# Moving the second product's seven small matrix products into one column group

## The chip, the cores and the metric

One core of one Trainium2 chip runs the whole program. The metric is device microseconds of one execution, as the median of several runs.

## The reference

```python
# x: (8, 4096, 192), weight: (8, 7)
w = softmax(weight, axis=-1)                        # 7 taps for each of 8 heads
out = einsum('hk,bskhg->bshg', w, x_unf)            # causal convolution along the sequence
# then, with x = out as (32768, 192), w_in: (192, 2048), w_out: (2048, 192)
h = x @ w_in
g = h * clip(h + 3.0, 0.0, 6.0) / 6.0
return g @ w_out                                    # (32768, 192), float32
```

A seven-tap convolution along the sequence is followed by two dense layers with a hard-swish gate between them.

## The kernel before, in words

The 32,768 tokens are cut into 32 blocks of 1,024, two halves of 512 tokens each. Block 0 has a form of its own. Blocks 1 to 31 each run `first_layer` and then `second_layer`; blocks 1 to 30 are the steady blocks, and block 31 takes the branches marked `last`. The convolution of a later block, on VectorE and ScalarE, is spread between the steps of the current one.

The first layer (`first_layer`, matmuls at L512) makes sixteen units of 128 hidden columns each. Each unit fills two PSUM banks; ScalarE (L303) and VectorE (L307) turn it into the gated values in the tile `g` and give the banks back. PSUM has eight banks, used as four slots of two.

The second layer (`second_layer`) multiplies `g` with `w_out`. The product is cut into seven smaller products by a Strassen-like scheme (`prod`, numbered 1 to 7: sums of blocks of `g` against sums of blocks of `w_out`). The result of one product has 96 rows, three thirds of 32. For products 1, 2, 4 and 5 two of the thirds are cut once more by the same scheme, into seven small products each; the remaining third is done plainly.

All these matmuls have 32 output rows, so TensorE runs them in four column groups, 0 to 3, side by side. Group j writes the 32 PSUM partitions from 32j on, called `first`, `second`, `third` and `fourth` in the code; such a strip of a bank is a quadrant here. The order is written out by hand as a plan of 80 steps per group. A plain matmul has 512 columns and takes two steps, a short one (of a small product) has 256 and takes one; each is an fp32 matmul and leaves two passes in the trace. These are the helpers:

- `plain(j, bank, n, q, chunks, start)` puts matmuls of product n, third q, into group j's strip of a bank, one for each of the eight chunks of `g`.
- `small(n, m, out, start, j)` puts the four short matmuls of small product m of product n.
- `level_two(n, p, order, j)` puts small products in the given order, into four strips of half a bank (`chains[j]`: A, E, B, C), and queues for each the copy that it needs: A to B after the first, B to C after the sixth, and copies to the SBUF tile of the product after the others.
- `fill(k)` puts k plain matmuls of the third third of product 5 into group 3, bank `a`.
- `do(t, fn)` queues work of the other engines (copies on ScalarE, sums on VectorE, transfers on GpSimd) at step t, half a step early. All streams are then sorted by step, and this is the order of the instructions on each engine; within one engine nothing overtakes.

The bank names: `x_, b`, `y_, c` and `a, _` are the three slots that the first layer gives back first, `f, h` the fourth. `x_` and `y_` hold the strips A, E and B, C of `level_two`. `b` collects products 6 and 3 on top of product 1 (and holds plain thirds early on), `c` product 7. Where one bank of PSUM is copied to another (`copy`, on ScalarE) matmuls go on adding to the copy. The framework sets the semaphores; a matmul waits for a copy or a sum by a count of the engine's finished instructions, and two instructions that touch one bank can be put in order in this way even where their partitions differ.

In the steady blocks before, the pieces of the second product stand in all groups: small products 1, 7, 2 and 4 in group 0, 5 in group 1, 3 in group 2 and 6 in group 3, with copies from strip to strip between them (`B2`, `C2`, `D2`), and its plain third in group 3. The plain third of product 4 stands in group 0, at the start of bank `b`.

Lines that matter: L512 first-layer matmuls, L640 second-layer matmuls, L637 the copies queued by `do(..., copy, ...)`, L730 to L735 the six copies of `level_two` (in the order first, second, sixth, fifth, seventh, third small product), L817 to L819 and L857, L858 the copies of product 2 to SBUF, L557 a negation on ScalarE ahead of an accumulating transfer, L588, L415 and L459 sums. L849 and L930 copy finished products, L1078 and L477 are the first multiplication of the next convolution and the first part of the split of `y`.

Of the kernel before, what the change touches and what calls it, by code (L numbers as in the profile page):

```python
# [25 lines left out]
def kernel(  # L26
# [16 lines left out]
    N = 512  # L43
    G = 2
    TB = G * N
    D2 = P // 2
# [41 lines left out]
    for base, dma in ((0, nc.scalar), (D2, nc.sync)):  # L88
        dma.dma_start(
            out=w_sb[base : base + D2],  # L90
            in_=weight.unsqueeze(1).to_broadcast([H, GJ, KC]),
# [126 lines left out]
    for n in range(AHEAD):  # L218
# [8 lines left out]
        out=e_sb[:], in0=w_sb[:], in1=mx[:].to_broadcast([P, KC]), op=ALU.subtract  # L227
# [54 lines left out]
    def take():  # L282
        return free_banks.pop(0)
# [72 lines left out]
    every = range(NP)  # L356
# [90 lines left out]
    def rows(q):  # L447
        return slice(q * QS, (q + 1) * QS)
# [9 lines left out]
    def add(out, x, y, op=ALU.add):  # L458
        nc.vector.tensor_tensor(out=out, in0=x, in1=y, op=op)  # L459
# [112 lines left out]
    halves = slice(0, TH), slice(TH, N)  # L572

    def four_parts(x):
        return [x[:, c::2, t] for t in halves for c in range(2)]
# [14 lines left out]
    def quarters(w):  # L590
        return [
            w_out[:, c::2, w, q * QS : (q + 1) * QS] for c in range(2) for q in range(2)
        ]
# [12 lines left out]
    def second_layer(i, between):  # L606
        last = i + 1 == NB
        ours = [free_slots.pop(0) for _ in range(3)]
        x_, b, y_, c, a, _ = (psum[:, 2 * n + k] for n in ours for k in range(2))
# [3 lines left out]
        copy = nc.scalar.copy  # L613
        m = slice(0, DH)
        lo, hi = halves
        both = nc.sync, nc.scalar
        first, second, third, fourth = (rows(q) for q in range(4))
        f, h = (psum[:, 2 * free_slots[0] + k] for k in range(2))
        end = h
        V = a[fourth]  # L620
        chains = {
            j: [bank[rows(j), t] for bank in (x_, y_) for t in halves] for j in (1, 2, 3)
        }
        A2, E2, C2, D2 = f[first, lo], f[second, hi], h[first, lo], h[third, hi]
        B2 = h[second if last else fourth, hi]
        j1 = 3 if last else 1
        late = {}

# [3 lines left out]
        def put(j, cost, fn):  # L632
            streams[j].append((clock[j], fn))
            clock[j] += cost

        def do(t, fn, *args, **kw):
            streams[3].append((t - 0.5, lambda: fn(*args, **kw)))  # L637

        def matmul(j, out, w, x, start):
            nc.tensor.matmul(  # L640
                out=out, lhsT=w, rhs=x, start=start, stop=True,
                tile_position=(0, j * QS), skip_group_check=True,
            )

        def plain(j, bank, n, q, chunks, start=False):
            x, w = prod[n]
            x = S3 if x is None else x
            for k, ch in enumerate(chunks):
                put(j, 2, lambda ch=ch, k=k: matmul(
                    j, bank[rows(j)], w_out[:, ch, w, q * QS : (q + 1) * QS], x[:, ch],  # L650
                    start and k == 0,
                ))
# [8 lines left out]
        def small(n, m_, out, start=False, j=3):  # L661

            x, w = prod[n]
            sums, ws = {
                1: (shared, w_s[:, 0]), 5: (s5, w_s[:, 1]), 2: (sums2, w_s[:, 2]),
                4: (sums4[0], w_s[:, 3]),
            }[n]
            x11, x12, x21, x22 = four_parts(x)
            z1, z2, z3, z4 = four_parts(sums)
            b11, t3, b21, b22 = quarters(w)  # L670
            t1, t2, t4 = (ws[:, k] for k in range(3))
            xm, wm = {
                1: (x11, b11), 2: (x12, b21), 3: (z4, b22), 4: (x22, t4),
                5: (z1, t1), 6: (z2, t2), 7: (z3, t3),
            }[m_]
            for u in range(NP // 2):
                put(j, 1, lambda u=u: matmul(
                    j, out, wm[:, u], xm[:, u], start and u == 0
                ))
# [16 lines left out]
        def fold(p, m136):  # L696
            add(p[second, hi], p[second, hi], p[second, lo])
            add(p[second, lo], m136, p[second, lo])
# [11 lines left out]
        def p2(r, t):  # L710
            return late["p2"][r, t]

        def p3(q):
            if last:
                plain_by_halves(q, 3, q, 0)
                plain_by_halves(q, 3, q, 1)
            else:
                plain(q, b, 3, q, in_fours)
# [6 lines left out]
        p4 = Fourth()  # L725

        def level_two(n, p, order, j=3):
            A, E, B, C = chains[j]
            steps = {
                1: lambda: copy(out=B, in_=A),  # L730
                2: lambda: copy(out=p()[first, lo], in_=A),
                6: lambda: copy(out=C, in_=B),
                5: lambda: copy(out=p()[second, lo], in_=E),
                7: lambda: copy(out=p()[second, hi], in_=C),
                3: lambda: copy(out=p()[first, hi], in_=C),  # L735
            }
            to = {1: A, 2: A, 6: B, 5: E, 7: C, 3: B, 4: C}
            for k in order:
                small(n, k, to[k], k in (1, 5), j)
                if k != 4:  # L740
                    late_by = {(1, 2): 8.1, (4, 2): 8.2 if last else 19.3}.get((n, k), 0.02 if n == 4 else 0)
                    do(clock[j] + late_by, steps[k])

        rest = 6, 2, 7, 5, 4, 3
        chunks, first_fill = list(every), [True]

        def fill(k):
            plain(3, a, 5, 2, [chunks.pop(0) for _ in range(k)], first_fill.pop() if first_fill else False)
# [2 lines left out]
            for ch in every[2:6]:  # L751
                by_half(3, (a, c)[t], 2, 2, ch, t)

        plain(0, b, 4, 2, every, True)
        small(2, 1, A2, True, 0)
        plain(0, c, 7, 0, every, True)
        small(2, 7, C2, False, 0)
        small(2, 2, A2, False, 0)
        plain(0, b, 6, 0, every)
        small(2, 4, C2, False, 0)  # L760
        p3(0)

        if last:
            plain(1, b, 1, 2, every, True)
            plain(1, c, 7, 1, every[:4], True)
            plain(1, a, 2, 2, every[:2], True)
            small(2, 6, B2, False, 1)
            plain(1, c, 7, 1, every[4:])
            small(2, 5, E2, True, 1)
            plain(1, b, 6, 1, every)  # L770
            plain(1, a, 2, 2, every[6:])
        else:
            level_two(1, lambda: p1, (1,), 1)
            plain(1, c, 7, 1, every[:4], True)
            level_two(1, lambda: p1, rest, 1)
            plain(1, c, 7, 1, every[4:])
            plain(1, b, 6, 1, every)
            small(2, 5, E2, True, 1)
        p3(1)

        level_two(4, lambda: p4, (1,), 2)
# [2 lines left out]
        level_two(4, lambda: p4, rest, 2)  # L784
        plain(2, c, 7, 2, every[ahead:])
        plain(2, b, 6, 2, every)
        small(2, 3, D2, False, 2)
        p3(2)

        if last:  # L790
            level_two(1, lambda: p1, (1,))
            fill(2)
            level_two(1, lambda: p1, rest)
            fill(4)
        else:
            plain(3, b, 1, 2, every, True)
            plain(3, c, 2, 2, every[:6], True)
            small(2, 6, B2, False)
            plain(3, c, 2, 2, every[6:])
            fill(4)  # L800
        level_two(5, lambda: late["p5"], (1,))
        fill(2)
        level_two(5, lambda: late["p5"], rest)
# [5 lines left out]
        assert clock == [80] * 4  # L809

        for t in halves:
            do(30 if t == hi else 29, copy, out=p4[third, t], in_=b[first, t])
        do(25.5, copy, out=p1[third], in_=b[second if last else fourth])
        do(20, copy, out=B2, in_=A2)
        do(31.9, copy, out=C2, in_=B2)
        do(39.6, copy, out=D2, in_=B2)
        do(40, lambda: copy(out=p2(second, hi), in_=C2))  # L817
        do(44, lambda: copy(out=p2(first, lo), in_=A2))
        do(44 if last else 64, lambda: copy(out=p2(second, lo), in_=E2))  # L819

        for t, job in between:
            do(t, job)
# [31 lines left out]
        if last:  # L854
            do(49, lambda: copy(out=late["p5"][third], in_=V))
        else:
            do(56.6, lambda: copy(out=p2(third, slice(0, N)), in_=c[fourth]))  # L857
        do(64.4, lambda: copy(out=p2(first, hi), in_=C2))  # L858
        if last:
            do(64.4, lambda: add(p2(third, slice(0, N)), a[second], p1[third]))  # L860
            for bank, t in ((a, lo), (c, hi)):
                do(64.4, lambda bank=bank, t=t: copy(out=bank[fourth, t], in_=p2(third, t)))
        do(64.4, lambda: fold(late["p2"], D2))
        whole = slice(0, 2 * QS if last else DH)
        do(64.6, lambda: add(late["p2"][whole], late["p2"][whole], p1[whole]))
        if last:
# [92 lines left out]
    with tc.manual_schedule():  # L959
# [4 lines left out]
            out=c_sb[:], in0=e_sb[:], in1=sm[:].to_broadcast([P, KC]), op=ALU.mult  # L964
# [14 lines left out]
        b = take()  # L979
        for cols in (N, N, N // 2):  # L980

            nc.tensor.matmul(  # L982
                out=psum[:, b, 0:cols], lhsT=zeros[:, 0:P], rhs=zeros[:, 0:cols],
# [59 lines left out]
        n = 3  # L1043
        for slot, (c, group) in enumerate(parts):
            first = slot < len(early)
# [27 lines left out]
        late = ctx.enter_context(tc.tile_pool(name="late", bufs=1, reuse_waits="tile"))  # L1073
# [60 lines left out]
        last = ctx.enter_context(tc.tile_pool(name="last", bufs=1, reuse_waits="tile"))  # L1134
# [55 lines left out]
```

## Time and profile before

| what | value |
|---|---|
| median of 3 runs | 2195.47 us (2195.26 to 2195.56) |
| the profiled execution | 2195.6 us, its span 2193.8 us |
| TensorE matmuls | 2188.3 us busy, 100% of the span |
| VectorE, ScalarE, GpSimd busy | 89%, 56%, 54% of the span |
| granted TensorE clock | 1.00 |
| one second layer, 1479.66 to 1514.21 | 34.55 us: VectorE busy 30.39, ScalarE 20.57, GpSimd 12.96 |
| one first layer, 1446.80 to 1479.66 | 32.86 us: VectorE busy 30.16, ScalarE 17.38, GpSimd 24.26 |

The profile is one execution. Starts and ends are microseconds from its beginning. Matmul ends in it are modelled, since matmuls are pipelined, so starts are compared with starts. The chain is the list of work that ended last, followed back from the end; a wait names the instruction that released it.

### The profile page before, as it was taken

The numbers are of one execution on the slowest core, as the hardware profiler recorded it, in microseconds if no ns is written. First come the engines' busy times: TensorE is split into PE (matmuls) and PEld (weight loads), VectorE is DVE, ScalarE is ACT, GpSimd is POOL, SyncE is SP. The second block draws the span as 40 slices with busy tenths as digits, with TensorE's granted clock in tenths as the row PEclk, the third lists the DMA queues.
The fourth block names the chain that finished last, engine by engine and source line by source line (L and its number), as shares of the span: only waits on it lengthen the run. The fifth ranks groups of instructions, "written<-read, shape, count | busy, mean of one in ns | idle before, by whom it ended". The sixth has DMA issues, their size and how long they took to land.

```text
span 2193.8 us, 53991 instructions
## 1 busy us (share of the span) xinstructions
PE 2188.3 (100%) x22984; PEld 1501.9 (68%) x22984; DVE 1953.5 (89%) x1956; ACT 1230.1 (56%) x1800; POOL 1178.8 (54%) x1028
## 2 busy tenths in 40 slices
PE   9999999999999999999999999999999999999999
PEld 4467776677766677766777667776667776677766
DVE  8888998898998889988899888999888998899977
ACT  7355565554555655555546555455565555554654
POOL 2456654565544666445655456554456554565544
PEclk9999999999999999999999999999999999999999
DMA  6277778777778777797777878777877778777776
GB/s 159 60 138 146 147 147 151 141 146 145 148 139 157 141 139 146 147 159 131 147 147 145 148 145 145 145 146 145 159 135 139 147 148 154 135 147 144 135 143 112
DMA packets 352434, 312.59 MB, mean 142 GB/s; under 512 B 211904, under 2 KB 264640, under 8 KB 352192
## 3 DMA queue, kind: packets, MB, share of 16 engines
q0 software_dynamic: 114640, 233.87, 59.3%
q1 hardware_dynamic: 235624, 74.66, 16.9%
q8 instruction: 180, 2.95, 0.6%
q10 hardware_dynamic: 1928, 0.59, 0.1%
q14 instruction: 62, 0.51, 0.1%
HBM read 31.72 MB, written 25.17 MB: 26 GB/s over the span
## 4 chain that ended last, share of the span: by engine, by line
PE 100%; DVE 0%; issue 0%
PE psum L640 49%; PE psum L512 46%; PE psum L297 2%; PE psum L342 2%; PE psum L974 0%; PE psum L982 0%; PE psum L895 0%; DVE zeros L111 0%; DVE shared L922 0%; DVE x L96 0%; DVE half L233 0%; DVE bias_e L150 0%; DVE bias_e L149 0%
## 5 line engine op out<-in xcount | busy, mean ns | idle before, releaser
L640 PE MATMUL psum<-g,w_out 128*32 128x512 f32 (+1 forms) x5960 | 922.8, 503 | 0.0
L303 ACT ACTIVATE g<-psum,half 128x1024 f32<-128x1024 f32 (+1 forms) x528 | 574.4, 1092 | 485.6 <-PE psum L512 485.6
L307 DVE SCALAR_TENSOR_TENSOR g<-g,psum 128x1024 f32<-128x1024 f32 (+1 forms) x528 | 608.2, 1180 | 106.4 <-ACT g L303 106.1
L640 PE MATMUL psum<-s,w_out 128*32 128x512 f32 (+1 forms) x3024 | 657.9, 585 | 0.0
L640 PEld LDWEIGHTS psum<-g,w_out 128*32 128x32 f32 x5960 | 375.0, 110 | 248.9 <-issue 116.0
L512 PE MATMUL psum<-y_own,w_in 64*128 64x512 f32 x4464 | 515.1, 388 | 0.0
L512 PE MATMUL psum<-y_other,w_in 64*128 64x512 f32 x4464 | 510.9, 386 | 0.0
L512 PEld LDWEIGHTS psum<-y_own,w_in 64*128 64x128 f32 x4464 | 415.8, 184 | 112.1 <-issue 26.0
L512 PEld LDWEIGHTS psum<-y_other,w_in 64*128 64x128 f32 x4464 | 418.1, 184 | 87.8
L588 POOL TENSOR_TENSOR shared<-g,shared 128x256 f32<-128x256 f32 x248 | 358.0, 1444 | 54.8 <-DVE g L307 29.0
L1080 DVE SCALAR_TENSOR_TENSOR y<-x,c_sb,y 128x1536 f32<-128x1536 f32 x186 | 334.7, 1799 | 0.2
L554 POOL DMA_DIRECT2D s<-g x123 | 147.1, 1198 | 266.4 <-PE psum L640 123.5
L640 PE MATMUL psum<-g,w_s 128*32 128x256 f32 x1488 | 282.3, 379 | 0.0
L640 PEld LDWEIGHTS psum<-s,w_out 128*32 128x32 f32 x3024 | 197.2, 110 | 74.0 <-issue 16.0
L554 POOL DMA_DIRECT2D g<-g x124 | 180.8, 1519 | 106.7 <-DVE s L415 106.7
L640 PE MATMUL psum<-z,w_s 128*32 128x256 f32 x992 | 228.1, 379 | 0.0
L640 PE MATMUL psum<-z,w_out 128*32 128x256 f32 x992 | 227.2, 379 | 0.0
L459 DVE TENSOR_TENSOR g<-g 128x1024 f32<-128x1024 f32 x124 | 148.7, 1220 | 44.5 <-PE psum L640 44.5
L588 POOL TENSOR_TENSOR shared<-g 128x256 f32<-128x256 f32 x124 | 92.0, 742 | 171.4 <-DVE g L307 171.4
L640 PEld LDWEIGHTS psum<-g,w_s 128*32 128x32 f32 x1488 | 138.0, 110 | 42.7
L266 POOL DMA_DIRECT2D y_other<-y_own x90 | 48.0, 534 | 213.2 <-DVE shared L459 213.1
L554 POOL DMA_DIRECT2D z<-g x62 | 95.8, 1545 | 116.3 <-ACT z L557 116.3
(118 smaller groups left out, 2706.4 us busy)
## 6 DMA issues: line engine op xcount, KB each, us to landing
y_other<-y_own POOLq DMA_DIRECT2D x180, 384.0 KB, 8.1
g<-g POOLq DMA_DIRECT2D x124, 512.0 KB, 6.0
s<-g POOLq DMA_DIRECT2D x123, 512.0 KB, 6.4
z<-g POOLq DMA_DIRECT2D x62, 512.0 KB, 7.2
out_dram<-shared SPq DMA_DIRECT2D x376, 64.0 KB, 3.9
x<-in_x_dram SPq DMA_DIRECT2D x53, 388.5 KB, 5.7
z<-g SPq DMA_DIRECT2D x31, 512.0 KB, 3.3
stage<-in_moe_w_in_dram SPq DMA_DIRECT2D x16, 192.0 KB, 5.0
```

Of the source, the lines that this page charges most:

```text
L266: dma.dma_start(out=to[D2:P], in_=part[0:D2])
L297: nc.tensor.matmul(out=psum[:, b], lhsT=w[r], rhs=src, start=start, stop=stop, skip_group_check=onto,)
L303: nc.scalar.activation(r6, h, ACT.Relu, bias=half[:], scale=1.0 / 6.0)
L307: nc.vector.scalar_tensor_tensor(out=g_, in0=g_, scalar=1.0, in1=h, op0=ALU.min, op1=ALU.mult)
L342: lambda p=p: nc.tensor.matmul(out=bank[j * QS : (j + 1) * QS, tokens], lhsT=w_out[:, p, w, cols], rhs=x[:, p, tokens], start=(first and p ...
L459: nc.vector.tensor_tensor(out=out, in0=x, in1=y, op=op)
L512: nc.tensor.matmul(out=psum[:, 2 * slots[n] + k], lhsT=r32(w_in_parts[part][r, c, s]), rhs=r32(y_other[0][r, part, s] if group else y_own[ ...
L554: nc.gpsimd.dma_start(out=out, in_=x, accum_op=ALU.add)
L588: engine.tensor_tensor(out=o, in0=p, in1=q, op=op)
L640: nc.tensor.matmul(out=out, lhsT=w, rhs=x, start=start, stop=True, tile_position=(0, j * QS), skip_group_check=True,)
L1080: jobs.append(lambda k=k: nc.vector.scalar_tensor_tensor(out=y[:], in0=x[:, :, k : k + N], scalar=c_sb[:, k : k + 1], in1=y[:], op0=ALU.mu ...
```

## The change

In the steady blocks the seven small products of the second product all go to column group 0, from step 12 on, by `level_two` with strips in `f` and `h`. What stood there moves: the plain third of product 4 starts with two chunks in group 0, bank `x_`, and is copied to `a[fourth]`, where group 3 adds the other six; of the plain third of product 5 two chunks are done in group 1, and of that of product 2 two chunks in group 2, each in its own strip of bank `a`, with copies of 512 columns that carry the partial sums from strip to strip. In each group there are then 28 short matmuls; before there were 16, 32, 32 and 32. The last block keeps its order.

```diff
+        chains[0] = [bank[first, t] for bank in (f, h) for t in halves]
...
-        B2 = h[second if last else fourth, hi]
+        B2 = h[second, hi]
...
-                    late_by = {(1, 2): 8.1, (4, 2): 8.2 if last else 19.3}.get((n, k), 0.02 if n == 4 else 0)
+                    late_by = {
+                        (1, 2): 8.1, (4, 2): 8.2 if last else 19.3, (2, 2): 8, (2, 7): -0.05, (2, 5): 4,
+                    }.get((n, k), 0.02 if n == 4 else 0)
                     do(clock[j] + late_by, steps[k])
...
-        plain(0, b, 4, 2, every, True)
-        small(2, 1, A2, True, 0)
-        plain(0, c, 7, 0, every, True)
-        small(2, 7, C2, False, 0)
-        small(2, 2, A2, False, 0)
-        plain(0, b, 6, 0, every)
-        small(2, 4, C2, False, 0)
+        if last:
...
+        else:
+            plain(0, x_, 4, 2, every[:2], True)
+            plain(0, c, 7, 0, every[:4], True)
+            level_two(2, lambda: late["p2"], (1,), 0)
+            plain(0, c, 7, 0, every[4:])
+            level_two(2, lambda: late["p2"], rest[:5], 0)
+            plain(0, b, 6, 0, every)
+            level_two(2, lambda: late["p2"], rest[5:], 0)
         p3(0)
...
             plain(1, b, 6, 1, every)
-            small(2, 5, E2, True, 1)
+            plain(1, a, 5, 2, every[4:6])
         p3(1)
...
-        small(2, 3, D2, False, 2)
+        if last:
+            small(2, 3, D2, False, 2)
+        else:
+            plain(2, a, 2, 2, every[6:])
         p3(2)
...
             plain(3, b, 1, 2, every, True)
+            plain(3, a, 4, 2, every[2:])
             plain(3, c, 2, 2, every[:6], True)
-            small(2, 6, B2, False)
-            plain(3, c, 2, 2, every[6:])
-            fill(4)
+            fill(2)
+            chunks[2:4] = []
         level_two(5, lambda: late["p5"], (1,))
         fill(2)
...
-            do(30 if t == hi else 29, copy, out=p4[third, t], in_=b[first, t])
+            do(30 if t == hi else 29, copy, out=p4[third, t], in_=(b[first, t] if last else a[fourth, t]))
...
-        do(20, copy, out=B2, in_=A2)
-        do(31.9, copy, out=C2, in_=B2)
-        do(39.6, copy, out=D2, in_=B2)
-        do(40, lambda: copy(out=p2(second, hi), in_=C2))
-        do(44, lambda: copy(out=p2(first, lo), in_=A2))
-        do(44 if last else 64, lambda: copy(out=p2(second, lo), in_=E2))
+        if last:
...
+        else:
+            do(4.2, copy, out=a[fourth], in_=x_[first])
+            do(44.05, copy, out=a[third], in_=c[fourth])
+            do(52.1, copy, out=a[second], in_=a[fourth])
+            do(64.5, copy, out=a[fourth], in_=a[second])
...
-            do(56.6, lambda: copy(out=p2(third, slice(0, N)), in_=c[fourth]))
-        do(64.4, lambda: copy(out=p2(first, hi), in_=C2))
+            do(64.4, lambda: copy(out=p2(third, slice(0, N)), in_=a[third]))
+        if last:
+            do(64.4, lambda: copy(out=p2(first, hi), in_=C2))
...
-        do(64.4, lambda: fold(late["p2"], D2))
+        do(64.4, lambda: fold(late["p2"], D2 if last else chains[0][2]))
```

In the changed kernel all lines after L624 stand one to 22 lines further down: the second-layer matmuls are L641, the queued copies L638, those of `level_two` L731 to L736.

More of the change, by code (lines that the diff above doesn't have):

```diff
@@ L752, in last_third @@
                 by_half(3, (a, c)[t], 2, 2, ch, t)
-        plain(0, b, 4, 2, every, True)
-        small(2, 1, A2, True, 0)
-        plain(0, c, 7, 0, every, True)
-        small(2, 7, C2, False, 0)
-        small(2, 2, A2, False, 0)
-        plain(0, b, 6, 0, every)
-        small(2, 4, C2, False, 0)
+        if last:
+            plain(0, b, 4, 2, every, True)
+            small(2, 1, A2, True, 0)
+            plain(0, c, 7, 0, every, True)
+            small(2, 7, C2, False, 0)
+            small(2, 2, A2, False, 0)
+            plain(0, b, 6, 0, every)
+            small(2, 4, C2, False, 0)
+        else:
[4 more added lines that the diff above has]
+            level_two(2, lambda: late["p2"], rest[:5], 0)
+            plain(0, b, 6, 0, every)
+            level_two(2, lambda: late["p2"], rest[5:], 0)
         p3(0)
@@ L811, in second_layer @@
         for t in halves:
-            do(30 if t == hi else 29, copy, out=p4[third, t], in_=b[first, t])
+            do(30 if t == hi else 29, copy, out=p4[third, t], in_=(b[first, t] if last else a[fourth, t]))
         do(25.5, copy, out=p1[third], in_=b[second if last else fourth])
-        do(20, copy, out=B2, in_=A2)
-        do(31.9, copy, out=C2, in_=B2)
-        do(39.6, copy, out=D2, in_=B2)
-        do(40, lambda: copy(out=p2(second, hi), in_=C2))
-        do(44, lambda: copy(out=p2(first, lo), in_=A2))
-        do(44 if last else 64, lambda: copy(out=p2(second, lo), in_=E2))
+        if last:
+            do(20, copy, out=B2, in_=A2)
+            do(31.9, copy, out=C2, in_=B2)
+            do(39.6, copy, out=D2, in_=B2)
+            do(40, lambda: copy(out=p2(second, hi), in_=C2))
+            do(44, lambda: copy(out=p2(first, lo), in_=A2))
+            do(44, lambda: copy(out=p2(second, lo), in_=E2))
+        else:
[3 more added lines that the diff above has]
+            do(64.5, copy, out=a[fourth], in_=a[second])
         for t, job in between:
```

## The prediction

> **What bounds the kernel now.** I read the page's busy times and its chain first, then the chain in order of time, then who the TensorE waited for.
>
> ```profile
> PE 2188.3 (100%) x22984; PEld 1501.9 (68%) x22984; DVE 1953.5 (89%) x1956; ACT 1230.1 (56%) x1800; POOL 1178.8 (54%) x1028
> PE 100%; DVE 0%; issue 0%
> ```
> ```profile
> 1446.87 32.86 PE psum L512 x288
> 1479.73 34.55 PE psum L640 x290
> ```
> ```profile
> PE psum L982 <- DVE half L233: 1.5, 1, 1.5
> ```
>
> The kernel is one unbroken stream of matmuls. In the chain every steady block is 32.86 us of first layer (L512) and 34.55 us of second layer (L640), 67.41 together. The third fence is the whole answer to "what did TensorE wait for": 1.5 us at the start, nothing in the blocks. So every other engine has slack today, no gain can come from a wait removed, and a cost comes only from a new wait of TensorE, times 30 steady blocks.
>
> Within one second layer (the block whose L640 starts at 1479.66) I read the passes of the matmuls (each fp32 matmul leaves two records):
>
> ```profile
> 1484.85 0.38 PE L640 MATMUL psum<-shared,w_s 128*32 128x256 f32 x1
> 1484.85 0.59 PE L640 MATMUL psum<-g,w_out 128*32 128x512 f32 x1
> ...
> 1485.07 0.38 PE L640 MATMUL psum<-shared,w_s 128*32 128x256 f32 x1
> ...
> 1485.28 0.38 PE L640 MATMUL psum<-shared,w_s 128*32 128x256 f32 x1
> 1485.28 0.59 PE L640 MATMUL psum<-g,w_out 128*32 128x512 f32 x1
> ...
> 1486.36 0.38 PE L640 MATMUL psum<-shared,w_s 128*32 128x256 f32 x1
> ```
>
> Starts count here, not the modelled ends. A long pass follows its predecessor in the same column group after 0.429 us (eight passes from 1481.42 to 1484.85), a short one after 0.2157 (seven, 1484.85 to 1486.36). One step of the plan is one long pass or two short ones: 0.4290 or 0.4314. The groups run independently: the long group is not slowed by the short one beside it.
>
> **TensorE's own work.** The change keeps 80 steps in each group and 112 short matmuls in all; it moves them from 16, 32, 32 and 32 per group to 28 in each. A short matmul costs 0.4314 - 0.4290 = 0.0024 us more than its step, so the slowest group loses 4 x 0.0024 = 0.01 us per block, 0.3 us over 30 blocks. That is the whole gain: -0.3 us. The Trainium skill, TensorEngine Tiling (Array Packing), Instruction Overhead, speaks of some 60 cycles of overhead for each matmul; eight passes fewer at that price would be an estimated 0.2 us per block, 6 us in all. The rows above have a fixed cost of 0.0024 and not 0.025 per pass, so the measurement decides.
>
> **Operands needed earlier.** From the VectorE timeline of the same block: the gate of the last unit (L307, 1480.92 + 1.22) ends at 1482.14, and small product 1 of the second product needs it at step 12, 1484.85. The last S3 chunks (L415) end at 1484.41, and are now needed at steps 16 and 20 (1486.6, 1488.3) instead of 28. The first of the z sums (L588, the pair at 1486.71) ends at 1487.9, now needed at step 24 (1490.0). The z sum at 1488.99 ends at 1490.2, now needed at step 36 (1495.2) instead of 60. The smallest cover is 2.1 us: cost nothing. The orders of VectorE, GpSimd and SyncE are the same instruction by instruction, so no DMA and no queue but ScalarE's and TensorE's is moved.
>
> **ScalarE.** Per block four copies of 512 columns come in (nearest row: L637 z<-psum 32x512, 0.58 us) and one copy of 256 goes (0.34), three copies more. ScalarE is busy 20.57 of the 34.55 us, so the sum fits; what counts is where it is dense. TensorE waits on ScalarE's count at certain matmuls, and the order of the changed kernel as built shows these waits. I compared each with the ScalarE row that it needs, shifted by what is now queued ahead:
> - step 20 (groups 1, 2), second of the two L732 copies: now 1487.54, one 0.37 copy ahead makes 1487.91; due 1488.30.
> - step 44, group 0, p1's copy into the bank (1497.05 + 0.57) and group 3, L731 of product four (1497.92): both 0.34 later, 1497.97 and 1498.27; due 1498.60.
> - step 68, group 3, L734: 1508.03 becomes 1508.41; due 1508.95.
> - three of the new copies: the one at 4.2 ends by 1483.0 and is first awaited at step 16 (1486.6); the one at 52.1 ends 1503.9 (behind L557, 1502.32 + 0.96 + 0.57), due at step 60, 1505.5; the one at 64.5 ends 1509.6 (fourth behind L1078), due at step 76, 1512.4.
>
> These keep 0.33 us or more. After a ScalarE write the weight load of a waiting matmul starts 0.06 us (L987 to L974 at 6.13) to 0.18 us (L1012, ending 13.03, to L297 at 13.21) later, and the matmul 0.03 after its load. So they cost nothing, the 0.33 with the least cover: at the upper latency 0.12 remains.
>
> **The one that does not fit: step 48.** As built, group 3's matmul at step 48 (`fill(2)` into bank `a`, fourth quadrant) waits for ScalarE's new copy `a[third] <- c[fourth]`, queued at 44.05, because both write bank `a`. Before, a `fill(2)` stood at step 48 too, but no copy wrote that bank ahead of it. This is ScalarE's stretch of before:
>
> ```profile
> 1495.43 0.36 ACT L735 COPY z<-psum 32x256 f32<-32x256 f32 x1 [0.18 <-PE psum L640]
> 1495.81 0.37 ACT L735 COPY shared<-psum 32x256 f32<-32x256 f32 x1
> 1496.09 1.05 ACT L557 ACTIVATE s<-g 128x1024 f32<-128x1024 f32 x1
> 1497.05 0.57 ACT L637 COPY psum<-z 96x512 f32<-96x512 f32 x1
> 1497.56 0.36 ACT L731 COPY shared<-psum 32x256 f32<-32x256 f32 x1
> 1497.94 0.34 ACT L637 COPY psum<-psum 32x256 f32<-32x256 f32 x1
> 1498.32 0.36 ACT L817 COPY shared<-psum 32x256 f32<-32x256 f32 x1
> 1498.70 1.06 ACT L557 ACTIVATE s<-g 128x1024 f32<-128x1024 f32 x1
> 1499.67 0.35 ACT L818 COPY shared<-psum 32x256 f32<-32x256 f32 x1
> 1500.66 0.34 ACT L730 COPY psum<-psum 32x256 f32<-32x256 f32 x1 [0.65 <-PE psum L640]
> ```
>
> The first row is released by TensorE at step 36; from there ScalarE is solid to 1500.02 and has 0.65 us free before step 48's copy. After the change three copies stand at step 36 instead of two (product two's comes in), one psum copy goes (D2), and the 512 copy stands at the end. Start to start by the rows above: 0.38 + 0.38 (three copies) + 0.28 (L557) + 0.96 (the 512 copy from z) + 0.51 (product four) + 0.38 (product two's copy at 40) + 0.28 to 0.38 (L557) + 0.97 (copy at 44) + 0.38, and 0.57 for the new copy: 5.09 to 5.19 from 1495.43. Group 0's release may come up to 0.04 earlier than group 2's did, so the copy ends between 1500.48 and 1500.62; I take 1500.55. With 0.10 for latency and load the matmul starts at 1500.65. It is due at 1479.66 + 0.04 (group 3's first passes) + 48 x 0.429 + 4 x 0.0024 = 1500.31. Group 3 is late by 0.34 us per block.
>
> Behind it in TensorE's queue stand the matmuls of step 50 for groups 0 to 2, due at 1501.17: they keep their time. Group 3 has 32 full steps left and nothing to catch up with, and the next first layer starts when the last group is through. So the block ends 0.34 later: 30 x 0.34 = 10.2 us. Bounds: earliest copy and 0.06 of latency, 0.23 per block; latest copy, 0.18 and a whole weight load (PEld, 0.11 us), 0.60. I stay near the middle because a plain ScalarE write released the 0.06 row.
>
> **Sum.** The profiled execution took 2195.6 (span 2193.8 and 1.8 around it), 0.1 above the median of 2195.47. With +10.2 - 0.3 = +9.9 I get 2205.4 from the median. By the bounds: 2202.1 to 2213.2.
>
> **Rivals.**
> - *The copy lands in time* (not slower). Place: step 48; price nothing; it decides when the chain above ends before 1500.21 to 1500.25, 0.3 us sooner than I add up. For it: only one row (L557 after L817, 0.28 or 0.38) is open; against: the other spacings are rows of just these instructions, and they repeat from block to block. The time is 2195.47 - 0.3 = 2195.2. The Trainium skill, PSUM — Partial Sum Buffer, PSUM bank collisions raise a hardware error, would guard by bank and quadrant, which makes the wait needless here, the copy being in the third quadrant and the matmul in the fourth; the built order waits nonetheless, and no row of before can tell, since no wait was late there. Chance 0.11.
> - *The hold reaches all groups or a second wait bites.* If the blocked queue also starves groups 0 to 2 (weight loads go out at the start of the pass before, so theirs for step 50 at 1500.75, little later than the release at about 1500.6), or step 44's 0.33 is used up as well, another 0.2 to 0.4 us per block is lost: 2211 to 2217. Against it: half a microsecond of queued work in each group. Chance 0.07.
> - *Short matmuls cost far more than 0.0024* and the balance pays: at ten times the row's price 3 us come back. The stall then gives 2202, without it 2192.5. The starts in the rows speak against it. Chance of the faster side 0.01.
>
> **How the numbers follow.** The stall at step 48 has 0.81 and gives 2205.4. The range 2201 to 2212 holds nearly all of it and of the lower part of the second rival; what is left out is the copy in time and the upper tail. A change of 0.2%, 4.4 us, is what a measurement of this kernel can tell from none; it takes 0.157 us per block, below my lower bound. Slower: 0.81 + 0.07 less a little for a chain that is shorter than its bound, 0.87; same 0.12; faster 0.01.
>
> **What would show it.** In the chain in order of time L641 stands at about 34.88 us per steady block and L512 at 32.86. TensorE or its weight loads get a wait, some 30 times, on ScalarE's 32x512 psum copy (L638). In ScalarE's timeline that copy, the tenth item after step 36's release, ends about 20.9 us after the block's second layer began; group 3's next starts shift by a third of a microsecond against the other groups and the shift stays to the end of the block. The idle VectorE time of 0.8 us before L459 at 1505.80 absorbs its own 0.4. It is wrong if L641 stays at 34.54, which makes it the first rival, or if TensorE waits elsewhere, at step 20, 44 or 68.

## The result and the profile after

The changed kernel takes 2205.44 us (median of 6 runs, 2205.33 to 2205.65) against 2195.51 before (6 runs): 9.93 us more, a ratio of 1.0045 with a 95% interval of 1.0032 to 1.0058.

The page's busy times and the head of its chain, and then two pieces of the chain in order of time (start, length, what):

```profile
PE 2197.9 (100%) x22984; PEld 1556.8 (71%) x22984; DVE 1953.6 (89%) x1956; ACT 1290.5 (59%) x1890; POOL 1176.5 (53%) x1028
PE 100%; DMA 0%; DVE 0%; ACT 0%; issue 0%; ACTq 0%
```
```profile
1114.95 32.87 PE psum L512 x288
1147.82 34.86 PE psum L641 x288
```

TensorE is still busy all the time by the page. The second layer has grown from 34.55 to 34.86 us, the first from 32.86 to 32.87. Taken from the starts in the trace and averaged over the steady blocks it is 34.551 to 34.862 and 32.862 to 32.871: 30 x 0.311 + 31 x 0.009 = 9.6 us. The spans differ by 10.0; the other 0.4 lies ahead of the first steady block (its L512 begins at 98.93 instead of 98.56), a stretch that the change does not touch and that begins anywhere from 98.4 to 99.6 in the experiments.

ScalarE in the block whose second layer starts at 1147.75, from step 36 on:

```profile
1163.47 0.36 ACT L735 COPY shared<-psum 32x256 f32<-32x256 f32 x1 [0.21 <-PE psum L641]
1163.85 0.36 ACT L736 COPY z<-psum 32x256 f32<-32x256 f32 x1
1164.24 0.36 ACT L736 COPY shared<-psum 32x256 f32<-32x256 f32 x1
1164.51 1.05 ACT L557 ACTIVATE s<-g 128x1024 f32<-128x1024 f32 x1
1165.47 0.57 ACT L638 COPY psum<-z 96x512 f32<-96x512 f32 x1
1165.99 0.74 ACT L732 COPY shared<-psum 32x256 f32<-32x256 f32 x2
1166.64 1.05 ACT L557 ACTIVATE s<-g 128x1024 f32<-128x1024 f32 x1
1167.71 0.36 ACT L734 COPY shared<-psum 32x256 f32<-32x256 f32 x1
1168.10 0.56 ACT L638 COPY psum<-psum 32x512 f32<-32x512 f32 x1
1168.80 0.34 ACT L731 COPY psum<-psum 32x256 f32<-32x256 f32 x1
```

ScalarE works without a pause for 5.2 us, and the new copy `a[third] <- c[fourth]` (the row at 1168.10) ends 20.90 us after the second layer's start; the matmul that waits for it was due at 20.65. From here on, times of a block are counted from the start of its second layer. Who TensorE's matmuls waited for, the whole answer, shows nothing of this:

```profile
PE psum L1004 <- DVE half L233: 1.5, 1, 1.5
PE psum L996 <- ACT diag L1009: 0.3, 1, 0.3
```

Both rows belong to the start of the kernel. The held group is one of four, and while the other three work TensorE is not idle, so the profile has no wait of the matmuls to list. The list for the weight loads has no row for it either: ahead of the held load they are idle for only 0.13 us (20.819 to 20.950), and the list leaves out idle times of 0.15 us and less. In e1 and e3 below this idle time is longer, and the row is there. The starts of the changed kernel show where the groups part, at the end of the second layer:

```profile
1181.75 0.60 PE L641 MATMUL psum<-s,w_out 128*32 128x512 f32 x3
1182.09 0.59 PE L641 MATMUL psum<-g,w_out 128*32 128x512 f32 x1
1182.62 0.50 PE L512 MATMUL psum<-y_own,w_in 64*128 64x512 f32 x2
```

The three passes on `s` are the last of groups 0 to 2. Group 3's last, on `g`, starts 0.34 later than the first of them, alone, and the next first layer follows it at its usual 0.52. Before, the four last passes of a block started within 0.06 us.

In the starts of that block group 3's pass at step 48 comes at 20.952, where 20.654 was due (its start in e1, e2 and e4 below): 0.298 late. Its weight load goes out at 20.950, 0.05 after the copy's end. The pass after it follows at 0.453 instead of 0.429, 0.024 more. From there group 3 keeps a lag of 0.322 to the end; groups 0 to 2 keep their times to within a nanosecond (20.684, 21.113, 21.542 for group 0, as in e4). With the 0.010 that the balance gives back the block is 0.312 longer.

### The profile page after: what moved, and what is told of

Read it like the earlier page. It is cut to its first block, busy times and chain, and to the rows that moved or that the text cites. A ratio compares the mean times of both kernels' runs of the same rounds, so it can differ in the third digit from the quotient of the medians.

```text
span 2203.8 us, 54141 instructions
## 1 busy us (share of the span) xinstructions
PE 2197.9 (100%) x22984; PEld 1556.8 (71%) x22984; DVE 1953.6 (89%) x1956; ACT 1290.5 (59%) x1890; POOL 1176.5 (53%) x1028
## 4 chain that ended last, share of the span: by engine, by line
PE 100%; DMA 0%; DVE 0%; ACT 0%; issue 0%; ACTq 0%
PE psum L641 49%; PE psum L512 46%; PE psum L297 2%; PE psum L342 2%; PE psum L996 0%; DMA w_sb<-in_weight_dram 0%; PE psum L917 0%; ACT diag L1009 0%; DVE shared L944 0%; ACT e_sb L229 0%; DVE c_sb L985 0%; DVE e_sb L226 0%; DVE sm L984 0%; DVE sm L982 0%; DVE mx L224 0%
## 5 line engine op out<-in xcount | busy, mean ns | idle before, releaser
L641 PE MATMUL psum<-g,w_out 128*32 128x512 f32 (+1 forms) x5960 | 979.1, 503 | 0.0
L641 PE MATMUL psum<-s,w_out 128*32 128x512 f32 (+1 forms) x3024 | 557.1, 585 | 0.0
L641 PEld LDWEIGHTS psum<-g,w_out 128*32 128x32 f32 x5960 | 405.0, 110 | 184.6 <-issue 55.2
L512 PE MATMUL psum<-y_own,w_in 64*128 64x512 f32 x4464 | 515.3, 388 | 0.0
L512 PE MATMUL psum<-y_other,w_in 64*128 64x512 f32 x4464 | 510.9, 386 | 0.0
L512 PEld LDWEIGHTS psum<-y_own,w_in 64*128 64x128 f32 x4464 | 415.8, 184 | 112.4 <-issue 26.0
L512 PEld LDWEIGHTS psum<-y_other,w_in 64*128 64x128 f32 x4464 | 418.1, 184 | 87.8
L641 PE MATMUL psum<-g,w_s 128*32 128x256 f32 x1488 | 286.3, 379 | 0.0
L641 PEld LDWEIGHTS psum<-s,w_out 128*32 128x32 f32 x3024 | 161.5, 110 | 81.5 <-issue 53.7
L459 DVE TENSOR_TENSOR g<-g 128x1024 f32<-128x1024 f32 x124 | 148.8, 1220 | 44.2 <-PE psum L641 44.1
L641 PEld LDWEIGHTS psum<-g,w_s 128*32 128x32 f32 x1488 | 138.0, 110 | 60.5 <-issue 9.2
L641 PE MATMUL psum<-z,w_s 128*32 128x256 f32 x992 | 178.9, 379 | 0.0
L641 PE MATMUL psum<-z,w_out 128*32 128x256 f32 x992 | 178.9, 379 | 0.0
L588 DVE TENSOR_TENSOR g<-g 128x1024 f32<-128x1024 f32 x124 | 149.1, 1222 | 2.1
```

Of the source, the lines that this page charges most:

```text
L512: nc.tensor.matmul(out=psum[:, 2 * slots[n] + k], lhsT=r32(w_in_parts[part][r, c, s]), rhs=r32(y_other[0][r, part, s] if group else y_own[ ...
L588: engine.tensor_tensor(out=o, in0=p, in1=q, op=op)
L641: nc.tensor.matmul(out=out, lhsT=w, rhs=x, start=start, stop=True, tile_position=(0, j * QS), skip_group_check=True,)
```

## The experiments

The theory: the time is group 3's wait at step 48 for the end of that ScalarE copy, because both touch bank `a`. The rivals: it is a price of the added copies (three more per block, bank to bank, beside running matmuls), or of the short matmuls all standing in one group. All kernels were timed beside the kernel before on the same chip. The ends of the copy and the lengths of the two layers are means over the steady blocks, from the starts in each trace, in us; "no wait" means that the copy's target is in another bank, as in e4.

| kernel | copy ends at | second layer | first layer | median, and that of before beside it |
|---|---|---|---|---|
| before | (no copy) | 34.551 | 32.862 | |
| changed | 20.90 | 34.862 | 32.871 | 2205.44, 2195.51 |
| e4, other bank | 20.91 | 34.541 | 32.906 | 2197.02, 2195.79 |
| e1, copy sooner | 20.51 | 34.541 | 32.906 | 2196.69, 2195.79 |
| e2, two copies later | 20.13 | 34.541 | 32.906 | 2196.80, 2195.79 |
| e3, one copy more | 21.29 | 35.256 | 32.868 | 2217.49, 2195.79 |
| e5, group 3 longer | no wait | 34.571 | 32.862 | 2196.65, 2195.90 |
| e6, group 0 ahead | no wait | 34.571 | 32.862 | 2195.56, 2195.90 |
| e7, one cut | no wait | 34.546 | 32.881 | 2195.53, 2195.70 |
| e8, three cuts | no wait | 34.556 | 32.871 | 2195.49, 2195.70 |

**The wait alone, ScalarE untouched (e4).** The partial sum goes to a strip of another bank.

```diff
-            plain(2, a, 2, 2, every[6:])
+            plain(2, f, 2, 2, every[6:])
...
-            do(44.05, copy, out=a[third], in_=c[fourth])
+            do(44.05, copy, out=f[third], in_=c[fourth])
...
-            do(64.4, lambda: copy(out=p2(third, slice(0, N)), in_=a[third]))
+            do(64.4, lambda: copy(out=p2(third, slice(0, N)), in_=f[third]))
```

> The partial sum of product 2's plain third goes to the third strip of bank f instead of bank a; ScalarE's order and times stay as they are, the copy still ends at 20.90 us, but group 3's matmul at step 48 shares no bank with it and gets no wait. Theory: L641 34.54 us, 2195.2 us. Rival (a late ScalarE copy, or copies from bank to bank beside running matmuls, slow TensorE by themselves): 34.86 and 2205.4 us.

ScalarE's rows around the copy (second layer from 1144.02) and two pieces of the chain:

```profile
1163.99 0.36 ACT L734 COPY shared<-psum 32x256 f32<-32x256 f32 x1
1164.38 0.56 ACT L638 COPY psum<-psum 32x512 f32<-32x512 f32 x1
1165.03 0.34 ACT L731 COPY psum<-psum 32x256 f32<-32x256 f32 x1
```
```profile
1111.19 32.91 PE psum L512 x288
1144.09 34.54 PE psum L641 x291
```

The copy ends as late as in the changed kernel (20.91), all the copies are there, all 28 short matmuls of group 0 too, and the second layer is down to 34.541. Group 3's pass at step 48 starts at 20.654, as it was due. Both rivals fall. The time, 2197.02, is 1.8 above what was expected; the chain says where most of it lies: the first layer went up to 32.91, which is 1.3 us in 30 blocks.

**The copy in time (e1, e2).** One moves the copy ahead of product 2's copy of step 44, the other takes two of product 2's copies out of the dense stretch.

```diff
-            do(44.05, copy, out=a[third], in_=c[fourth])
+            do(43.9, copy, out=a[third], in_=c[fourth])
```

> Theory (group 3's matmul at step 48 waits for the end of the copy into a[third]): the copy leaves ScalarE one 256-column copy (0.38 us) sooner, ends 20.42 to 20.52 us after the second layer begins instead of 20.90, and the matmul, due at 20.65, is 0 to 0.03 us late instead of 0.30. L641 34.54 to 34.57 us per steady block instead of 34.86; 2195.2 to 2196.5 us. Rival (the time lies in the three more ScalarE copies, or in 28 short matmuls running in group 0): all of these are still there, so 34.86 per block and 2205.4 us.

```diff
-                        (1, 2): 8.1, (4, 2): 8.2 if last else 19.3, (2, 2): 8, (2, 7): -0.05, (2, 5): 4,
+                        (1, 2): 8.1, (4, 2): 8.2 if last else 19.3, (2, 2): 25, (2, 7): -0.05, (2, 5): 17,
```

> Theory: two of product 2's copies (steps 40 and 44) go behind step 56.5, the copy into a[third] then ends near 20.1 us, half a microsecond before it is due, with its weight load on time. L641 34.54 us, 2195.2 us (before less 0.3). Nothing new is late: the moved copies fall into ScalarE's idle 0.8 us ahead of step 60. Rival (more copies or more short matmuls cost the time): 34.86 and 2205.4 us.

The copy ends at 20.51 and 20.13, the waiting pass starts at 20.654 in both, the second layer is 34.541 in both. In e1 the copy has 0.14 us to spare and that is enough. The wait is still built into both programs; it costs nothing when the copy is in time. In e1 the list of the weight loads' waits even names it:

```profile
PEld psum L641 <- ACT psum L638: 5.2, 30, 0.2
```

That is 0.17 us in each block, and the pass behind the load is still on time: such a row counts idle time of the weight loads, not time lost. Again the first layer is 32.906, so the times are 1.5 and 1.6 us above the 2195.2 of a copy in time, and e1's is 0.2 above the upper end of what was expected.

**One more copy ahead of it (e3).**

```diff
+            do(44.02, lambda: copy(out=p2(second, lo), in_=chains[0][1]))
             do(44.05, copy, out=a[third], in_=c[fourth])
```

> One needless 256-column copy (product 2's step-44 copy, done twice with the same data) stands just ahead of the copy into a[third]. Theory: the copy ends 0.37 to 0.39 us later and group 3 with it, one for one: L641 35.23 to 35.25 us, 30 x 0.38 = 11.4 us more, 2216.8 us. Rival (the loss is a fixed cost of the moved matmuls, ScalarE having slack): 34.86 and 2205.4 us.

The added row (L838) and the copy behind it (second layer from 1153.63), and the chain:

```profile
1173.98 0.36 ACT L838 COPY shared<-psum 32x256 f32<-32x256 f32 x1
1174.37 0.56 ACT L638 COPY psum<-psum 32x512 f32<-32x512 f32 x1
```
```profile
1153.70 35.26 PE psum L641 x288
```
```profile
PEld psum L641 <- ACT psum L638: 15.7, 30, 0.5
```

The third fence is the wait as the list of the weight loads has it here: 30 times, on just this copy. The copy ends 0.393 us later than in the changed kernel, and the second layer is 0.394 longer (35.256 against 34.862): one for one. Thirty blocks of it are 11.8 us; the median is 12.05 above the changed kernel's, in other runs, and 0.7 above what was expected.

**What the first layer does (e5, e6).** Without the wait all four groups end within 0.02 us, and each first layer is 0.044 us longer than before, 1.3 us in all. The extra time lies in the first eleven pairs of passes of the first layer: the 21st pass starts 2.437 us after the first instead of 2.397, and from the 23rd on both go in step. To see if the ends of the groups matter, e5 and e6 take the kernel of e4 (its three changed lines are not shown again) and cut plain matmuls of the steady blocks into halves, which makes a group longer by 0.0048 us for each:

```diff
-            plain(3, a, 5, 2, [chunks.pop(0) for _ in range(k)], first_fill.pop() if first_fill else False)
+            begin = first_fill.pop() if first_fill else False
+            for n in range(k):
+                ch = chunks.pop(0)
+                if last:
+                    plain(3, a, 5, 2, [ch], begin and n == 0)
+                else:
+                    for t in range(2):
+                        by_half(3, a, 5, 2, ch, t, begin and n == 0 and t == 0)
```

> On top of the kernel with the other bank (no wait at step 48): product 5's six plain matmuls in group 3 are cut into halves, so that group 3 has 40 short matmuls and the others 28. By the 0.0024 us of a short matmul group 3 then ends 0.03 us behind the others: L641 34.57 us. What is asked is where the 0.043 us comes from by which each first layer got longer (L512 32.906 against 32.862) in the three kernels without the wait. Theory: the four groups now end within 0.02 us of one another, and the first layer's start depends on that; with one group behind, L512 goes back toward 32.86, and the time stays near 2196.7. Rival (the waits and banks at the start of the first layer, which this edit leaves alone): L512 stays at 32.906, and the time is 0.9 us longer, 2197.7.

For e6 also, in `p3` (with `by_half` taking S3 where a product has no operand of its own):

```diff
-                plain(q, b, 3, q, in_fours)
+                if q:
+                    plain(q, b, 3, q, in_fours[:2])
+                    for ch in in_fours[2:]:
+                        for t in range(2):
+                            by_half(q, b, 3, q, ch, t)
+                else:
+                    plain(q, b, 3, q, in_fours)
```

> As the kernel with group 3 cut into halves, and six plain matmuls of product 3 in groups 1 and 2 cut as well: 28, 40, 40 and 40 short matmuls, so that group 0 ends 0.03 us ahead of the other three, as it did (by 0.04) before the change. L641 34.57 us. Theory (the spread of the ends sets the start of the first layer): L512 near 32.86, the time near 2196.7. Rival (waits or banks): L512 32.906, 2197.7 us.

The chain of e5, and of e6:

```profile
1143.22 34.57 PE psum L641 x282
1177.79 32.86 PE psum L512 x288
```
```profile
1142.79 34.57 PE psum L641 x329
1177.36 32.86 PE psum L512 x288
```

In both the first layer is back at 32.862, as before the change, and the second layer is longer by the 0.030 of six cuts. No wait and no bank of the first layer's start was edited, so that rival falls. The times follow only roughly (2196.65 and 2195.56, with blocks of equal length; e6 is 1.1 under what was expected): differences below 1 us are lost in what varies from execution to execution, and the chain is the better witness.

**How much spread (e7, e8).** On top of e4 again, only the last, or the last three, of group 3's plain matmuls are cut (`if last or len(chunks) > 0:` and `> 2` in place of `if last:`).

> The kernel with the other bank, and only the last plain matmul of group 3 cut into halves: 30 short matmuls there, 28 elsewhere, so group 3 ends 0.005 us later. L641 34.546 us. If that much spread is enough for the first layer's quick start, L512 is 32.862, a steady block takes 67.408 (before: 67.413) and the time is 0.1 to 0.2 us under that of before, which is less than can be told from no change. If the spread must be larger, L512 stays at 32.906 and the time near 2196.8 us. Rival to the whole spread theory (cutting matmuls of the last steps helps by itself, however many): 32.862 here as well, so this run alone does not tell that apart; it sizes the step.

> Three of group 3's plain matmuls cut: 34 short ones there, 28 elsewhere, group 3 ends 0.014 us later. L641 34.556 us. With the quick start of the first layer 67.418 us a block and a time equal to before within 0.2 us; without it 67.462 and 2196.9 us.

Group 3 longer by 0, 0.005, 0.014 and 0.029 us (e4, e7, e8, e5) gives a first layer of 32.906, 32.881, 32.871 and 32.862: it shrinks step by step, not at one point, and e7 came out at neither of the two values that were expected. A steady block is then 67.447, 67.427, 67.427 and 67.433, against 67.413 before. None of the kernels has shorter blocks than the kernel before; e7 and e8 measure the same as it (ratios 0.9998 and 0.9999, intervals from 0.9989 and 0.9990 to 1.0007 and 1.0008). With a cut the last passes of group 3 are also short ones, which is a rival to the spread. The kernel before has long last passes and spread ends, and has the quick start too, so the short pass is not needed for it. Nor is it enough: e5 and e8 run the same passes in group 3 from step 50 on and differ there only in how late they are (the last one starts at 34.262 and 34.246), and the first layers still differ.

## Why the prediction was right, point by point

- **TensorE's own work, -0.01 us per block.** Shown by e1, e2 and e4: 34.541 against 34.551. The starts of the last passes say the same: group 0 starts its last 0.03 later than before, the others 0.01 earlier, relative to the block's start.
- **ScalarE's sum.** The copy was to end 20.82 to 20.96 us after the second layer's start (1500.48 to 1500.62), 20.89 taken; it ended at 20.90. The open row was L557 behind the copy of step 40: that L557 started early (1166.64), but did not let the next copy begin before its own end, so 0.97 became 1.07 and the two differences cancelled.
- **Latency and load, 0.10 taken.** Measured 0.05 from the copy's end to the weight load and 0.002 from there to the matmul. The step that the sum did not have is the restart: the first pass of a group that had run dry takes 0.024 more. Together 0.322 of lag instead of 0.34.
- **Groups 0 to 2 keep their time.** Shown by the starts. The second rival, a starved queue, did not happen: their next weight loads stand behind the held one, and it went out 0.165 us before they were due (20.950, against 21.115 to 21.138, as in e4). In e3 the queue did hold them. There the held load goes out at 21.344 and theirs only behind it, at 21.350 to 21.364; their passes start on time, from 21.543 on, because a load goes out one pass ahead, and some 0.2 us of that were left. By these rows a longer hold should reach all four groups, as that rival says; none was tried.
- **The other waits.** At steps 20, 44 and 68 nothing is late: without the wait at step 48 the second layer is at its 34.541. The list of the weight loads has one more new row, 6.8 us on the sums of L415 in 23 blocks; it stands in e4 too, so it costs nothing.
- **The copy in time, as a rival.** Its mechanism is e1, and its 2195.2 was 1.5 us too low: the balance of short matmuls wins 0.010 us in the second layer and loses 0.044 in the first, by bringing the four ends together. That term was missing from the sum, where it is small, because the late group spreads the ends again (32.871): 0.3 us.
- **What was wrong.** A wait of TensorE or of its weight loads on the copy, "some 30 times", was to be seen in the profile. The wait is there (the load at 20.950 follows the copy's end by the same 0.05 us as in e1 and e3), but no list of the changed kernel names it, because the idle time ahead of the load is too short; the lists of e1 and e3 have it, 30 times. And since the sum came to +9.9 against a measured +9.93, it should be said that this closeness is partly luck: 0.5 us too much for latency and lag, 0.3 too little for the first layer, and 0.4 ahead of the first steady block that no term stands for.
- **Slips in the working.** The estimate of 0.2 us per block and 6 us in all counts eight passes fewer. In group 1, 2 or 3 four short matmuls, eight passes, give way to two plain ones, four passes, so four go, and at the price taken there it is 0.1 us and 3 us; the measured 0.010 is far from either. The due time adds up to 1500.30, not 1500.31 (the 20.654 of the runs is 1500.31 there), and the third rival with the stall to 2202.7, not 2202. None of these changes the forecast.
- **The bank and the quadrant.** e4 shows that the wait exists only because copy and matmul share a bank. Whether the chip would have needed it, the two being in different quadrants, was not tried: the wait alone was not taken away.

## What to carry to other kernels

Where an in-order engine feeds TensorE's plan, add up that engine's queue start to start from the last point where it was waiting, and compare the end with the step that needs it; an engine that is busy 60% of a stage can still be full in the 5 us that count. When TensorE runs several column groups, a held group makes the whole stage longer while the matmuls show no idle time at all, and a wait in the list of the weight loads need not cost anything (e1): look at the starts of each group's last passes, where a held group stands alone. If a copy cannot be sooner, put its target in a bank that no running matmul uses.

## What the runs showed of the hardware that was not expected

- The passes of the other column groups do not move when one is held for 0.3 us (or 0.7 in e3), and the lag of the held one stays until the stage ends. Their weight loads are not independent: in e3 they wait behind the held load, 0.23 us late, and only the pass that they are ahead covers it.
- A group that has run dry pays for the restart: 0.453 us for its first long pass (0.454 in e3) against 0.429.
- The start of a stage with another tiling depends on how the one before it ends: with four groups ending within 0.02 us the first eleven pairs of passes of the first layer take 0.044 us more than with one group 0.03 to 0.05 us away from the rest. More spread does not make it quicker still: with group 3 behind by 0.3 us (the changed kernel) and 0.7 (e3) the first layer is 32.871 and 32.868 against 32.862. The runs show that it is how the ends lie to one another that moves it; what in TensorE does it stays open.
